# Long convolution and spectral mix: the filter's second transform is moved in front of the first pair's ticks

## The chip, the cores and the metric

One core of a Trainium2 chip runs the whole kernel. The metric is the device time of one execution in microseconds (us), the median of several runs. A profile of one further execution is shown; its time is given beside it. TensorE (PE in the profile, PEld for its weight loads) multiplies, VectorE (DVE) and ScalarE (ACT) empty PSUM and do elementwise work, GpSimd (POOL) and SyncE (SP) mainly issue DMAs.

## The reference

```python
# x: (8, 5696, 128), h: (5696, 128), w_r, w_i: (64, 128, 128), w_ch: (128, 128)
L = 2 * S
Yf = np.fft.rfft(x, n=L, axis=1) * np.fft.rfft(h, n=L, axis=0)[None]
x = np.fft.irfft(Yf, n=L, axis=1)[:, :S, :]          # causal long convolution
X = np.fft.rfft(x, axis=1)                           # spectral mix on the first 64 modes
Yr = einsum(Xr, w_r) - einsum(Xi, w_i);  Yi = einsum(Xr, w_i) + einsum(Xi, w_r)
u = x + np.fft.irfft(Y, n=S, axis=1)
out = u + np.maximum(u @ w_ch, 0.0)
```

## The kernel before, in words

**Tiling.** A sequence of 5696 is cut as 64 x 89 (J = 64, NQ = 89). A transform has two steps. The first step runs along the 89 and gives NK = 90 modes k. The second step runs along the 64, one small matrix per mode, out of the table `M`. The eight batches go in four pairs (`g_` = 0 to 3). The 90 modes of a pair go in NT = 23 ticks of KT = 4 modes (the last has 2).

**One pair.** First come 32 tiles of the first transform (`a_tile`, j = 0 to 31): four matmuls of x against the table F each, and one eviction of 128x720 from PSUM into `As`, on ACT or on DVE. The function `share` gives each eviction to the engine with the smaller sum of estimated costs. For the first pair all 32 tiles stand together; of a later pair the first six are spread over the last ticks of the pair before (`border`), and the other 26 follow those ticks. Then come the ticks (`tick`, t = 0 to 25), in which several steps overlap:

- `second(t)`: 16 matmuls `As` x `M` into two of the PSUM banks 0 to 3.
- `products(t)`: the product with the filter, `Hs`, on DVE. In most ticks ACT first copies the two banks to SBUF (`Xs`) and DVE multiplies from there.
- two ticks later (LC = 2), four matmuls `U` x `Wc` (banks 4 to 6), two ACT evictions into a room `Zs` or `Zt`, and one DMA of 256 KB from there to DRAM (`zscr`), issued on SP. The DMA has to land before the room is filled again.
- three ticks later (LM = 3), eight matmuls `Zs` x `G` (bank 7), which gather the 64 modes of the spectral mix.

During a pair's ticks GpSimd also issues the loads of x for the next pair (`x_load`, at the even ticks 2 to 16), and DVE puts them in place (`x_place`).

**Two forms of tick.** In the pairs after the first, `twin` makes the second transforms of two ticks stand together (32 matmuls in a row), and in every fourth tick (`straight`) DVE multiplies directly from PSUM without an ACT copy. The first pair has neither. It uses 6 rooms for its z tiles at the start, where the two middle pairs use 10 throughout.

**The filter.** Its first transform is made ahead of x (`Ah`). Its second transform is `filter_tick(t)`: 16 matmuls `Ah` x `M` with 64 columns, one eviction 128x512 to `Hs`, two DMAs of 64 KB on SP that copy `Hs` to its second plane with the partition halves exchanged, and after each odd t up to 11 one DMA of a piece of the table `G`, on SP too. Of the 23, the first six (LH = 6) are made among the first pair's tiles of x, one behind each third tile from j = 11 on. The others are made in the first pair's ticks, `filter_tick(t + 6)` at the end of tick t, in PSUM banks 2 and 3. That is why `second` of the first pair has only banks 0 and 1 until the filter is done.

**Queues.** Every engine runs its list strictly in the order in which the functions above are called. The recorder adds semaphore waits for data and for reuse. A DMA takes the next slot of a ring and waits until the slot's last DMA has landed; the ring of the `Hs` copies ("s") has 8 slots, that of the z writes ("z") 8, that of the `G` pieces 16. SP waits in its own list, so a copy that cannot go yet holds the z writes behind it.

**Fillers.** `keep(n, bank)` issues n matmuls whose result is not used: 12 behind the first pair's tiles, and 8 behind each of its ticks 0 and 1.

All matmuls are recorded at line 320, all DMAs at line 317, the evictions at 308 and 312 (plain, ACT and DVE) and 310 and 314 (scaled, ACT and DVE), the products at 592 and 600, `x_place` at 356. The profile's groups are therefore told apart by their tiles.

Of the kernel before, what the change touches and what calls it, by code (L numbers as in the profile page):

```python
# [123 lines left out]
def bass_long_conv_fft__then__afno_spectral_mix_kernel(nc, x, h, moe_w_r, moe_w_i, moe_w_ch, out):  # L124
# [8 lines left out]
    NP = B // 2  # L133
    KT = 4
    NT = (NK + KT - 1) // KT
# [15 lines left out]
    c, s = np.cos(th), np.sin(th)  # L151
# [75 lines left out]
    g_sb = at("G", GW, F16, a_g)  # L227
    ah_sb = at("Ah", HW, F16, a_g)
    NU, NXS, NZ, NZX = 3, 2, 6, 10
    NZS = [NZ] + [NZX] * (NP - 2) + [8]  # L230
    NZL = NZS[-1]
    a_st = take((2 * NU + NXS + NZ) * 2048)
    h_in = at("Hin", J * D, F16, a_st)
# [194 lines left out]
    def share(n):  # L428
        a, v = load["scalar"] + COST[n][0], load["vector"] + COST[n][1]
        e = "scalar" if a <= v else "vector"  # L430
        load[e] = min(a, v)
        return e
# [19 lines left out]
             [bank(t), bank(t + 1)], [("as", j)], 1.0 / 64, eng=eng, after=once(("hp", j), HP))  # L452


    def filter_tick(t, banks, eng="vector"):
        n = len(ticks[t])
        hb = banks
        for i, k in enumerate(ticks[t]):
            for r in range(2):
                for dh in range(2):  # L460
                    mm(pv(hb[dh], i * DH, [[1, DH]]),
                       ap(m_sb, MW, J * dh, J, k * 3 * J + (J if r == 0 else 0) + dh * J, [[1, P]]),
                       ap(ah_sb, HW, J * dh, J, (2 * k + r) * DH, [[1, DH]]), r == 0, r == 1,
                       AHT + mtok(k) + [("ag", k)], [bank(hb[dh])])
        lo, hi = KT * t * D, (KT * t + n) * D
        old = once("xr", [t_ for r_ in XR for t_ in r_]) if t == 0 else []
        evac(h_sb[:, lo:hi], pv(hb[0], 0, [[DH, n], [512, 2], [1, DH]]), [bank(hb[0]), bank(hb[1])], [("h", t, 0)],
             eng=eng, after=old)
        for p0, p1 in ((0, J), (J, 0)):
            dma("sync", h_sb[p0:p0 + J, HW + lo:HW + hi], h_sb[p1:p1 + J, lo:hi], "s", [("h", t, 0)], [("h", t, 1, p0)])  # L470
        if t % 2 and t // 2 < NG:
            s0, s1 = t // 2 * GP, min(t // 2 * GP + GP, NS)
            dma("sync", g_sb[:, s0 * P:s1 * P], bass.AP(c_g, s0 * P, [[GW, P], [1, (s1 - s0) * P]]), "c", (),
                [("g", t // 2)], after=[("ag", k) for k in range(s0, s1)])
# [62 lines left out]
    def keep(n, b0):  # L537
        for i in range(n):
            mm(pv(b0 + i % 2, 0, [[1, 2 * NK]]), f1_sb[:, 0:P], f1_sb[:, :], True, True, [("f1",)], [bank(b0 + i % 2)])

    LC, LM, LH = 2, 3, 6
    ZR = 96
    XBANKS = [bank(0), bank(1), bank(2), bank(3)]

    def with_h_at(g_, t):
        return g_ == 0 and t + LH < NT

    onchip = {}

# [5 lines left out]
        return e  # L555

    def twin(g_, t):
        return g_ > 0 and t % 2 == 1

    def straight(g_, t):  # L560
        return g_ > 0 and t % 4 == 3

    def slot_of(g_, t):
        if g_ == 0 or t == 0:
            return XSLOT[(t + 1) % 2 if t and not with_h_at(g_, t) else 0]
        return XSLOT[((t - 1) // 4 + t) % 2]

    def second(g_, t):
# [32 lines left out]
              bk + [("h", t, 0), ("h", t, 1, 0), ("h", t, 1, J)], [("u", i)])  # L601

    Z_OLD = [("ag", k) for k in range(NS, NS + 8 * (NZX - NZ))]
    XPLACE = [9, 10, 12, 15, 16, 18, 20, 22], [9, 10, 13, 14, 17, 18, 20, 22]

    def zroom(g_, s_):
        return (s_ - 2 * NZ) % NZX if g_ == 0 and s_ >= 2 * NZ else s_ % NZS[g_]

    def xtok(n):
        return [("xt", n, p_) for p_ in range(2)]  # L610
# [1 line left out]
    def tick(g_, t):  # L612
        if g_ + 1 < NP:
            for i in range(2 * XC):
                if t == XPLACE[g_ > 0][i]:
                    x_place(i, x_st[i], xtok(i))
        with_h = with_h_at(g_, t)
        if t < NT:
            of_two = t > 0 and twin(g_, t - 1)
            if not of_two and not (g_ == 0 and t > LC):  # L620
                second(g_, t)
            products(g_, t, slot_of(g_, t))
            if twin(g_, t):
                second(g_, t + 1)
                if straight(g_, t):
                    copied(g_, t + 1, slot_of(g_, t + 1))
        drain = list(border[t]) if t in border and g_ + 1 < NP else []
        if drain and t >= NT:
            j, sl, e = drain.pop(0)
            a_tile(j, [sl], e)  # L630
        if g_ + 1 < NP and t % 2 == 0 and 0 < t <= 4 * XC:
            i = t // 2 - 1
            x_load(g_ + 1, i, x_st[i], xtok(i), [("u", t % NU)] + AST)
        if LC <= t < NT + LC:
            s_ = t - LC
            n = len(ticks[s_])
            i, zi = s_ % NU, zroom(g_, s_)
            zb = [turns("z", ZBANK) for b in range(2)]
            for b in range(2):
                for r in range(2):  # L640
                    mm(pv(zb[b], 0, [[1, n * D]]), (W1, W2)[r], u_s[i][:, r * 1024 + b * 512:r * 1024 + b * 512 + n * D],
                       r == 0, r == 1, [("u", i), ("wc",)] + ([("u0", i)] if s_ == 0 and b else []), [bank(zb[b])])
                evac(bass.AP(z_s[zi], b * D, [[1024, P], [2 * D, n], [1, D]]),
                     pv(zb[b], 0, [[D, n], [1, D]]), [bank(zb[b])], [("zs", zi, b)], eng="scalar",
                     after=once(("zx", zi, b), Z_OLD) if zi >= NZ else ())
            zo = (g_ * NK + KT * s_) * P * 256
            dma("sync", bass.AP(zs, zo, [[256, P], [P * 256, n], [1, 256]]),
                bass.AP(z_s[zi], 0, [[1024, P], [256, n], [1, 256]]), "z",
                [("zs", zi, 0), ("zs", zi, 1)], [("zd", g_, s_)])
            if drain and t >= NT:  # L650
                j, sl, e = drain.pop(0)
                a_tile(j, [sl], e)
        if g_ == 0 and LC <= t < NT - 1:
            second(g_, t + 1)
        if LM <= t < NT + LM:
            s_ = t - LM
            zi = zroom(g_, s_)
            for b in range(2):
                for i, k in sorted(enumerate(ticks[s_]), key=lambda q: (s_ > 0 or q[1] != 1, q)):
                    if k % 2:  # L660
                        o, off, n, sl = pv(MB, b * P, [[1, P]]), (k + 1) // 2 * P, P, (k + 1) // 2
                    else:
                        ms, off = even[k]
                        n, sl = 2 * len(ms), 0
                        dims = [[M, 2]] if len(ms) == 1 else [[ms[1] - ms[0], 2], [M, 2]]
                        o = pv(MB, b * P + ms[0], dims)
                    mm(o, z_s[zi][:, i * 256 + b * P:i * 256 + b * P + P], g_sb[:, off:off + n],
                       k == 1 and b == 0, k == NK - 1 and b == 1, [("g", sl // GP), ("zs", zi, b)], [bank(MB)])
        if drain and t < NT + LM - 1:
            j, sl, e = drain.pop(0)  # L670
            a_tile(j, [sl], e)
        if with_h:
            filter_tick(t + LH, [2, 3])

    SLOTS = [0, 2, 4, 6]
    for j in range(32):
        a_tile(j, [turns("s", SLOTS)], "both" if j == 31 else share(720))
        if j >= 11 and j % 3 == 2 and (j - 11) // 3 < LH:
            b_ = turns("s", SLOTS)
            filter_tick((j - 11) // 3, [b_, b_ + 1], share(512))  # L680
    keep(12, turns("s", SLOTS))
    for g_ in range(NP):
        for t in range(NT + LM):
            tick(g_, t)
            if g_ == 0 and t < 2:
                keep(8, 4)
            assert g_ + 1 < NP or not wp
            if g_ == NP - 1 and t in early:
                pace[:] = [("u", min(t, NT - 1) % NU)]
                early[t]()  # L690
        evac(bass.AP(xt, 2 * g_ * XTW + M, [[B * XTW, P], [XTW, 2], [1, P]]), pv(MB, 0, [[P, 2], [1, P]]),
             [bank(MB)], [("xt", g_)], 1.0 / 64, eng="scalar", after=[("ag", k) for k in range(NS + 2 * XN, NK)])
        evac(bass.AP(xt, 2 * g_ * XTW, [[B * XTW, P], [XTW, 2], [1, M]]), pv(MB, M, [[P, 2], [1, M]]),
             [bank(MB)], [("xtn", g_)], -1.0 / 64, eng="vector" if g_ + 1 == NP else "scalar", after=[("ag", k) for k in range(NS + 2 * XN, NK)])
        if g_ + 1 < NP:
            for j in range(6, 32):
                a_tile(j, [(4, 6, 0, 2)[(j - 7) % 4] if j > 6 else 0], "both" if j == 31 else (A, V)[(j - 6) % 9 % 2])
                if j == 31:
                    keep(8, 6)
                if wp and j % 2 == 1:  # L700
                    dst, src_, ring, tok = wp.pop(0)
                    dma("gpsimd", dst, src_, ring, (), [tok], after=[("as", j)])
# [189 lines left out]
```

## Time and profile before

| | |
|---|---|
| median of 3 runs | 384.91 us (384.59 to 386.44) |
| profiled execution, its own time | 385.34 us |
| its span from first to last instruction | 383.2 us |
| PE, DVE, ACT, POOL busy | 96%, 81%, 79%, 22% of the span |
| granted TensorE clock | 0.99 |
| DMA | 103.94 MB, mean 271 GB/s |

The busy shares are means over stages with different limits. A PE marked busy is not one at its peak, since a matmul that stands in the pipeline behind a wait counts too. A stage's own length, and which work comes back at which distance in it, tell more. Times in the views count from the first instruction. The first pair's second transform begins at 43.88 us, those of the next pairs at 109.12, 164.28 and 219.06 us.

### The profile page before, as it was taken

To read this page: it belongs to the slowest core of one execution; us is meant where nothing else is said; L and a number is where in the kernel's file an instruction comes from. 1 tells how busy PE (TensorE), PEld (TensorE's weight loads), DVE (VectorE), ACT (ScalarE), POOL (GpSimd) and SP (SyncE) were. 2 spreads that over 40 slices of the span, in tenths; PEclk is the share of its full clock that TensorE was granted. 3 is DMA by queue.
4 is the path that set the end of the run, shared out by engine and by line. 5 is a ranking of instruction groups with operands and counts; after the bars stand their busy time and mean duration, and the time that the engine had idled before them with its cause. 6 is when DMAs were issued, how large, how long until landed. Compare 5 with 4: busy or idle time off the path is not lost.

```text
span 383.2 us, 12588 instructions
## 1 busy us (share of the span) xinstructions
PE 366.0 (96%) x5392; PEld 283.7 (74%) x5392; DVE 310.5 (81%) x348; ACT 302.7 (79%) x488; POOL 82.5 (22%) x133
## 2 busy tenths in 40 slices
PE   7999899999989999989999999999999999999994
PEld 7998756666866666866667866668898988887873
DVE  6969888998888999998998888875447767776876
ACT  1359688898889997989997999995457676776785
POOL 8400022220552320733310411319200000000000
PEclk9999999999999999999999999997999999999999
DMA  7998469999699997999995859999999999999879
GB/s 149 194 283 339 138 125 291 273 244 261 96 138 210 226 249 220 101 133 204 263 257 164 87 167 370 334 327 388 402 402 398 414 405 406 412 405 378 359 279 356
DMA packets 86865, 103.94 MB, mean 271 GB/s; under 512 B 22638, under 2 KB 72430, under 8 KB 83330
## 3 DMA queue, kind: packets, MB, share of 16 engines
q1 hardware_dynamic: 62523, 67.73, 50.5%
q0 software_dynamic: 24288, 35.43, 44.1%
q8 instruction: 42, 0.69, 0.7%
q14 instruction: 12, 0.10, 0.1%
HBM read 70.61 MB, written 51.12 MB: 318 GB/s over the span
## 4 chain that ended last, share of the span: by engine, by line
PE 69%; ACT 10%; DMA 9%; DVE 6%; POOL 2%; issue 2%; SPq 0%; DVEq 0%; POOLq 0%
PE ps L320 69%; ACT As L310 6%; DMA Xr<-in_x_dram 4%; DMA ZT0b<-zscr 4%; POOL Xr L317 2%; DVE As L314 2%; DVE U L592 1%; ACT UT L308 1%; ACT R L826 1%; ACT Zt L308 1%; DVE Xin L356 1%; ACT Xs L308 1%; DVE U L600 1%; DVE O L827 1%; DVE UT L312 0%
## 5 line engine op out<-in xcount | busy, mean ns | idle before, releaser
L600 DVE TENSOR_TENSOR U<-Xs,Hs 128x2048 f16<-128x2048 f16 (+1 forms) x73 | 86.7, 1190 | 12.0 <-ACT Xs L308 10.4
L320 PE MATMUL ps<-U,Wc 128*128 128x512 f16 (+1 forms) x368 | 94.0, 376 | 0.0
L308 ACT CAST Xs<-ps 128x1024 f16<-128x1024 f32 (+1 forms) x77 | 75.0, 979 | 9.0 <-PE ps L320 7.4
L308 ACT CAST Zs<-ps 128x512 f16<-128x512 f32 (+1 forms) x134 | 70.6, 596 | 5.9 <-PE ps L320 5.8
L827 DVE TENSOR_TENSOR O<-ps,R 128x512 f32<-128x512 f32 x81 | 52.6, 686 | 20.5 <-ACT R L826 15.2
L826 ACT ACTIVATE R<-ps 128x512 f32<-128x512 f32 x96 | 51.0, 573 | 14.2 <-PE ps L320 13.7
L314 DVE TENSOR_SCALAR As<-ps 128x720 f16<-128x720 f32 (+1 forms) x64 | 53.2, 880 | 5.1 <-PE ps L320 3.4
L320 PE MATMUL ps<-F,Xin 128*128 128x180 f16 x512 | 52.3, 250 | 2.6 <-DVE Xin L356 1.2
L320 PE MATMUL ps<-As,M 64*128 64x128 f16 x1440 | 50.6, 217 | 4.2 <-DVE U L592 3.0
L320 PEld LDWEIGHTS ps<-As,M 64*128 64x128 f16 x1440 | 40.3, 94 | 17.9 <-issue 8.1
L310 ACT ACTIVATE As<-ps 128x720 f16<-128x720 f32 x68 | 48.0, 768 | 6.4 <-PE ps L320 5.6
L320 PE MATMUL ps<-WI,UT 128*128 128x256 f16 x360 | 52.0, 279 | 0.5 <-DVE O L827 0.4
L320 PEld LDWEIGHTS ps<-F,Xin 128*128 128x128 f16 x512 | 44.5, 155 | 9.5 <-DVE As L314 2.6
L320 PEld LDWEIGHTS ps<-U,Wc 128*128 128x128 f16 x368 | 28.7, 97 | 27.6 <-ACT Zs L308 4.4
L317 POOL DMA_DIRECT2D Xt<-in_x_dram x48 | 26.0, 545 | 104.6 <-PE ps L320 100.2
L308 ACT CAST UT<-ps 128x712 f16<-128x712 f32 x40 | 30.0, 752 | 18.8 <-PE ps L320 17.8
L320 PEld LDWEIGHTS ps<-WI,UT 128*128 128x128 f16 x360 | 39.3, 152 | 4.4 <-issue 2.1
L320 PE MATMUL ps<-IBs,C 128*128 128x356 f16 x128 | 40.1, 323 | 0.6
L320 PEld LDWEIGHTS ps<-G,Zs 128*128 128x128 f16 x524 | 27.4, 96 | 11.7
L600 DVE TENSOR_TENSOR U<-ps,Hs 128x2048 f16<-128x2048 f32 x15 | 34.3, 2284 | 0.0
L320 PE MATMUL ps<-G,Zs 128*128 128x128 f16 (+2 forms) x524 | 32.6, 192 | 0.0
L320 PE MATMUL ps<-F 128*128 128x180 f16 x280 | 27.7, 254 | 2.5 <-DMA F<-cF 2.5
(86 smaller groups left out, 506.1 us busy)
## 6 DMA issues: line engine op xcount, KB each, us to landing
out_dram<-O SPq DMA_DIRECT2D x39, 512.0 KB, 11.4
zscr<-Zs SPq DMA_DIRECT2D x64, 256.0 KB, 6.8
Xt<-in_x_dram POOLq DMA_DIRECT2D x24, 320.0 KB, 7.0
zscr<-Zt SPq DMA_DIRECT2D x24, 256.0 KB, 6.6
W<-wscr POOLq DMA_DIRECT2D x4, 1024.0 KB, 8.9
M<-cM POOLq DMA_DIRECT2D x5, 720.0 KB, 20.5
ZT0a<-zscr SPq DMA_DIRECT2D x3, 1024.0 KB, 14.0
Hs<-Hs SPq DMA_DIRECT2D x44, 64.0 KB, 5.8
```

The costliest lines, as they stand in the source:

```text
L308: R.add(e, lambda h_: h_.copy(dst, src), reads, writes, after=after)
L310: R.add(e, lambda h_: h_.activation(dst, src, COPY, scale=scale), reads, writes, after=after)
L314: R.add(e, lambda h_: h_.tensor_scalar_mul(dst, src, scale), reads, writes, after=after)
L317: R.add(eng, lambda h_: h_.dma_start(dst, src), reads, writes, ring=ring, after=after)
L320: R.add("tensor", lambda h_: h_.matmul(o, l, r, start=st, stop=sp), reads, writes)
L356: R.add("vector", lambda e: e.tensor_copy(bass.AP(x_sb, i * XN * XS, [[XW, NQ], [XS, XN], [1, D]]), bass.AP(src, 0, [[XB, NQ], [D, XN], [1 ...
L592: R.add("vector", lambda e, b=b, s_=s_: e.tensor_tensor(bass.AP(u_s[i], b * 512, [[2048, P], [1024, 2], [1, n * D]]), s_, hv, MULT), [tok, ...
L600: R.add("vector", lambda e: e.tensor_tensor(uv, src, hv, MULT), bk + [("h", t, 0), ("h", t, 1, 0), ("h", t, 1, J)], [("u", i)])
L826: R.add("scalar", lambda e: e.activation(rv, src_r, RELU), bk, [("r", i % NR)], after=once(("r", i % NR), G_ALL + XTT + [("y", 0), ("y", 1 ...
L827: R.add("vector", lambda e: e.tensor_tensor(ov, src_u, rv, ADD), bk + [("r", i % NR)], [key + (h_,)], after=once(key, old))
```

## The change: what it does

All 23 filter ticks are now made among the first pair's 32 tiles of x: two at a time behind tiles 5, 7, 10, 12, 15, 17, 20, 22, 24, 27 and 29, and the last behind tile 30. Their evictions go to ACT or DVE by `share`, as before. No filter tick is left in the ticks, so banks 2 and 3 are free there, and the first pair's ticks take the later pairs' form: `twin`, `straight`, the same order of PSUM slots, the same places for x, 10 rooms for z. The fillers behind ticks 0 and 1 go, and those behind the tiles are 8 instead of 12.

```diff
-    NZS = [NZ] + [NZX] * (NP - 2) + [8]
+    NZS = [NZX] * (NP - 1) + [8]
...
-    LC, LM, LH = 2, 3, 6
+    LC, LM = 2, 3
...
-    def with_h_at(g_, t):
-        return g_ == 0 and t + LH < NT
...
     def twin(g_, t):
-        return g_ > 0 and t % 2 == 1
+        return t % 2 == 1
     def straight(g_, t):
-        return g_ > 0 and t % 4 == 3
+        return t % 4 == 3
     def slot_of(g_, t):
-        if g_ == 0 or t == 0:
-            return XSLOT[(t + 1) % 2 if t and not with_h_at(g_, t) else 0]
+        if t == 0:
+            return XSLOT[0]
         return XSLOT[((t - 1) // 4 + t) % 2]
...
-    XPLACE = [9, 10, 12, 15, 16, 18, 20, 22], [9, 10, 13, 14, 17, 18, 20, 22]
+    XPLACE = [9, 10, 13, 14, 17, 18, 20, 22]
     def zroom(g_, s_):
-        return (s_ - 2 * NZ) % NZX if g_ == 0 and s_ >= 2 * NZ else s_ % NZS[g_]
+        return s_ % NZS[g_]
...
-            if not of_two and not (g_ == 0 and t > LC):
+            if not of_two:
                 second(g_, t)
...
-        if g_ == 0 and LC <= t < NT - 1:
-            second(g_, t + 1)
...
-        if with_h:
-            filter_tick(t + LH, [2, 3])
     SLOTS = [0, 2, 4, 6]
+    done = 0
     for j in range(32):
         a_tile(j, [turns("s", SLOTS)], "both" if j == 31 else share(720))
-        if j >= 11 and j % 3 == 2 and (j - 11) // 3 < LH:
+        due = NT if j == 30 else max(0, j - 2) * NT // 28 // 2 * 2
+        while done < due:
             b_ = turns("s", SLOTS)
-            filter_tick((j - 11) // 3, [b_, b_ + 1], share(512))
-    keep(12, turns("s", SLOTS))
+            filter_tick(done, [b_, b_ + 1], share(512))
+            done += 1
+    keep(8, turns("s", SLOTS))
     for g_ in range(NP):
         for t in range(NT + LM):
             tick(g_, t)
-            if g_ == 0 and t < 2:
-                keep(8, 4)
```

More of the change, by code (lines that the diff above doesn't have):

```diff
@@ L452, in a_tile, with filter_tick @@
              [bank(t), bank(t + 1)], [("as", j)], 1.0 / 64, eng=eng, after=once(("hp", j), HP))
-    def filter_tick(t, banks, eng="vector"):
+    def filter_tick(t, banks, eng):
         n = len(ticks[t])
@@ L614, in tick @@
             for i in range(2 * XC):
-                if t == XPLACE[g_ > 0][i]:
+                if t == XPLACE[i]:
                     x_place(i, x_st[i], xtok(i))
-        with_h = with_h_at(g_, t)
         if t < NT:
             of_two = t > 0 and twin(g_, t - 1)
-            if not of_two and not (g_ == 0 and t > LC):
+            if not of_two:
                 second(g_, t)
```

## The prediction, made before the changed kernel was run

> **What bounds the kernel now.** I read the busy time by windows first, with a window for the first pair's tiles and one for each pair from its first `second` to the next pair's.
>
> ```profile
> core 0: us, PE busy (x) PEld busy (x) DVE busy (x) ACT busy (x) POOL busy (x), PEclk, DMA share, GB/s
> 27.96:43.88 15.92, 15.76 (x236) 13.78 (x237) 14.58 (x19) 14.54 (x20) 0.00 (x0) 1.00 0.78 284
> 43.88:109.12 65.24, 63.34 (x1048) 42.72 (x1050) 56.48 (x66) 55.88 (x87) 17.41 (x28) 1.00 0.93 203
> 109.12:164.28 55.16, 53.10 (x768) 37.74 (x769) 50.98 (x49) 50.81 (x82) 17.17 (x29) 1.00 1.02 193
> 164.28:219.06 54.78, 52.82 (x769) 37.73 (x770) 50.99 (x49) 50.80 (x82) 15.53 (x26) 1.00 0.97 190
> ```
>
> The first pair takes 65.24 us, the next two 55.16 and 54.78. The clock is 1.00 in all, so the 10 us are work and order, not the clock. The timeline of PE shows where they lie. Three excerpts follow: first-pair ticks with a filter tick, first-pair ticks without one, and two ticks of the second pair.
>
> ```profile
> 57.28 0.41 PE L320 MATMUL ps<-Ah,M 64*128 64x64 f16 x16
> 57.62 1.04 PE L320 MATMUL ps<-U,Wc 128*128 128x512 f16 x4
> 58.59 0.62 PE L320 MATMUL ps<-As,M 64*128 64x128 f16 x16
> 59.14 0.50 PE L320 MATMUL ps<-G,Zs 128*128 128x2 f16 x8
> 59.57 0.41 PE L320 MATMUL ps<-Ah,M 64*128 64x64 f16 x16
> ...
> 86.44 1.02 PE L320 MATMUL ps<-U,Wc 128*128 128x512 f16 x4
> ...
> 88.28 1.02 PE L320 MATMUL ps<-U,Wc 128*128 128x512 f16 x4
> ...
> 119.59 1.07 PE L320 MATMUL ps<-As,M 64*128 64x128 f16 x32
> 120.59 1.04 PE L320 MATMUL ps<-U,Wc 128*128 128x512 f16 x4
> ...
> 123.11 1.07 PE L320 MATMUL ps<-As,M 64*128 64x128 f16 x32
> ```
>
> The first column is the start. A tick with a filter tick comes back after 59.57 - 57.28 = 2.29 us, one without after 88.28 - 86.44 = 1.84, and in the twin form two ticks after 123.11 - 119.59 = 3.52, or 1.76 each. PE stands nearly closed up in the first, so the filter's matmuls there lie on the path.
>
> The tiles of x are different: both eviction engines are full there, as the timelines of ACT and DVE show.
>
> ```profile
> 28.55 14.68 ACT L310 ACTIVATE As<-ps 128x720 f16<-128x720 f32 x20 [3.12 <-PE ps L320]
> ...
> 33.18 0.69 DVE L312 CAST Hs<-ps 128x512 f16<-128x512 f32 x1
> 33.96 0.91 DVE L314 TENSOR_SCALAR As<-ps 128x720 f16<-128x720 f32 x1
> 34.78 0.68 DVE L312 CAST Hs<-ps 128x512 f16<-128x512 f32 x1
> ```
>
> ACT runs 20 evictions without a gap, DVE alternates with gaps under 0.1 us. PE could do a tile in 4 x 0.078 = 0.31 us (the spacing of the filler matmuls, 2.35 us for 30 weight loads), but the tiles come at 0.397 (12 tiles in 32.73 - 27.97 = 4.76 us). The evictions set this stage.
>
> **What leaves the ticks.** Filter ticks 6 to 22 leave 17 ticks of the first pair: 17 x (2.29 - 1.76) = 9.0 us. The six ticks that had none gain 6 x (1.84 - 1.76) = 0.5. The rest is the start, where the first pair has two fillers of 0.79 us, filter ticks and waits between its first `second` and its second `U,Wc` block (43.88 to 50.60, 6.7 us) and the second pair does the same in 4.5 us (109.12 to 113.58). Three filter ticks of that stretch are counted already. The windows give the total without such counting: 65.24 - 55.16 = **10.1 us less** (10.5 by the third pair). The work of the two pairs in that window is otherwise the same: as many x loads, z writes, placed pieces, tiles and pieces of w.
>
> **What the tiles of x get.** Sixteen full filter ticks and one of half size. Five groups of one filter tick and three tiles take 7.60 us (32.73 to 40.33 in the same timeline), 1.52 each; less 3 x 0.397 = 1.19 that is 0.33 for a filter tick. 16.5 x 0.33 = **5.4 us more**. Bounds: if `share` fills both engines evenly, a filter eviction costs what the two do side by side. ACT takes 0.54 for a 128x512 (1.08 for two z evictions) and DVE 0.69, together one in 0.30, which gives 5.0. If PE with its two banks per filter tick becomes the longer part, a filter tick costs what it costs in the ticks without the twin form, 2.29 - 1.84 = 0.45, which gives 7.4. I take 0.33, since it is measured in this stage with the same neighbours. So the first `second` comes at 43.88 + 5.4 = 49.3.
>
> **What the table M allows.** The filter reads M earlier. Its six pieces are issued at 10.69 to 13.32 and land 18.1, 19.3, 20.5 up to 25.7 us later: the first at 28.8, the second at 30.5, the last at 39.0. Filter ticks 0 and 1 now stand behind six tiles, at 27.97 + 6 x 0.397 = 30.4. Tick 3, which needs the second piece, comes at 27.97 + 8 x 0.397 + 3 x 0.33 = 32.1, and tick 18, which needs the last, at about 45. No wait; its cost would be at most the 1.6 us by which the first piece is ahead, should its order change.
>
> **What moves on SP.** Of the 46 copies of `Hs` 30, issued from 51.71 on, and the last two of the six G pieces move in front of the first z write. A pair of copies takes 1.13 us of SP, a G piece 0.64 with its gap, as the timeline of SP has it.
>
> ```profile
> 51.71 1.13 SPq L317 DMA_DIRECT2D Hs<-Hs  x2
> ...
> 55.01 0.59 SPq L317 DMA_DIRECT2D G<-cG  x1
> ```
>
> All of them: 23 x 1.13 + 6 x 0.64 = 29.8 us. The first copy follows its first matmul by 33.91 - 32.73 = 1.2 us, so SP starts at 31.5 and is free at 61.3 if nothing else holds it. The ring of 8 does hold it wherever a copy takes over 8 x 0.565 = 4.5 us to land. By the rows of the tile `Hs`, copies issued from 31 to 50 us land after 1.9 to 5.4 (median 3.1), those from 51 to 87, beside loads of x and z writes, after 4.8 to 8.2 (median 6.3).
>
> ```profile
> DMA to landing us min/median/max: 1.9/3.1/5.4
> DMA to landing us min/median/max: 4.8/6.3/8.2
> ```
>
> Ten copies at 5.4 while M arrives (0.67 each), twenty at SP's own 0.565, sixteen beside the x loads at 5.6 (0.70), somewhat under the 6.3 since no z writes are out then: 29.2 in place of 26.0, so SP is free at about 64.5. The first z write, which in the second pair goes 4.6 us into the pair, goes 15 us into it. Ten rooms make that free up to a point: the eleventh z tile is evicted 129.56 - 109.12 = 20.4 us into the pair, here at 69.7. The first write lands at 64.5 + 3.3 (the 51.15 one took 3.3) = 67.8. That cover is 1.9 us deep; at the 7.1 that is the median of the second pair's z writes the stall is 1.9. ACT would wait there, and behind it the copies for DVE. I take 0 and keep 1.9 for the range. The products do not wait: a tick's copies go out every 1.3 us or so from 31.5 on, the ticks come every 1.76 from 49.3 on.
>
> How copies fare beside long transfers decides the depth of that cover. The copy issued at 33.91 took 5.4 and landed at 39.3, just behind the last piece of M at 39.0: beside a long transfer of the other queue a copy waits. [...]
>
> **Without cost.** Four fillers fewer behind the tiles: they end at 43.73, before the last eviction of `As` at 43.82, so nothing stood behind them. The fillers in ticks 0 and 1 are in the 10.1 already. The second and third pair run at clock 1.00 without them.
>
> **Sum.** -10.1 + 5.4 = -4.7 us. The profiled execution took 385.34, so 380.6 on its scale. It lay 0.43 above the median of 384.91; on the median's scale the forecast is **380.2 us**. What follows only moves forward: the later pairs and the output stage hang on the pair before, not on absolute times.
>
> **Rivals.**
>
> *The z writes come late (slower).* If all 46 copies land in L us with L over 4.5, the ring sets their pace: SP is free at 31.5 + 3.8 + 46 L / 8, the first z write lands 3.3 later, and the stall at the eleventh z tile is 5.75 L - 31.1. It starts at L = 5.4, eats the 4.7 us at L = 6.2, and at L = 7.0 is 9.2 us: 389.4. For it: 6.3 is the median beside x loads, and 8.2 occurs. Against: until the x loads begin, some 5 us into the ticks, the bus has only M's end, copies and G, and copies in such a stretch (41.4 to 50) landed within 3.2. Chance 0.12, half of it beyond "no change".
>
> *The tiles pay more.* Filter ticks come in twos with one eviction each and hold two of four PSUM slots. At 0.45 each the gain is 10.1 - 7.4 = 2.7: 382.2. For it: PE's own 0.31 + 0.34 per tile and filter tick is close to the evictions' 0.70, so each waits for the other at times. Against: the measured 0.33. Chance 0.13.
>
> *The first pair does not reach 55.2 because of its transfers.* DMA share by length is 0.93 x 65.24 = 60.7 in the first pair and 1.02 x 55.16 = 56.3 in the second: copies and G are worth 4.4 us of the bus. About half of them now fall into the ticks, and the z writes in a block behind them. If the bus decides, 2.2 us come back through late pieces of x (DVE waits in `x_place`): 382.4; with the stall of 1.9 it is 384.3. Against: no wait for pieces of x stands among the second pair's waits, although its bus is as full. Chance 0.08.
>
> *It does not do what it says,* M being late or the order of slots holding the twin form back: about 384.9. Nothing in the trace asks for it; chance 0.02.
>
> **How the numbers follow.** The forecast has 0.65. The bound for a difference is 0.5%, 1.9 us: faster is under 383.0, slower over 386.8. Faster: 0.65, 0.11 of the dearer tiles and 0.04 of the transfers, 0.80. Slower: 0.06 of the late z writes and 0.01 of the rest, 0.07. No change: 0.13. The range: -10.5 + 5.0 with 0.9 for what the shorter start may add gives 384.91 - 6.4 = 378.5; above, 7.4 in the tiles and 1.9 of stall, 384.91 - 10.1 + 7.4 + 1.9 = 384.1. Outside lie the larger part of the late z writes and some below.
>
> **What would show it.** Right: the first `second` near 49.3, the next pair's near 104.4, two ticks in 3.5 us, copies of `Hs` in a row on SP to about 64, the first z write near there, and no wait on ACT before the eleventh z tile. Wrong: an ACT gap near 69.7 with a DMA `zscr` as releaser (late z writes); a first `second` after 51 (dearer tiles); DVE waiting for `Xt` (transfers).

## The result, and the profile after

The changed kernel takes 389.54 us (median of 4 runs, 389.04 to 389.87) against 384.87 us before (with one run more than in the table above): a ratio of 1.0103, 95% interval 1.0084 to 1.0122. The forecast was 380.2, so the sign is wrong. The profiled execution took 389.34 us, its span is 387.2. Among the profiled executions below, the output stage behind the pairs was longer than here by 6 us in e3, 4 in the repeat of the changed kernel and 2 in e2, so of these only the earlier stages are read.

Busy time by windows, after, with the same cuts as before: the tiles, then each pair from its first `second` on. The columns are the window, its length, busy time and instructions of each engine, granted clock, DMA share and GB/s.

```profile
27.89:50.13 22.24, 21.39 (x496) 18.15 (x497) 19.36 (x25) 19.12 (x31) 0.00 (x0) 1.00 0.75 260
50.13:112.16 62.03, 54.49 (x768) 38.13 (x768) 51.15 (x49) 50.77 (x82) 16.85 (x28) 0.94 0.94 195
112.16:167.31 55.15, 52.82 (x770) 37.73 (x770) 51.06 (x49) 50.80 (x82) 17.22 (x29) 1.00 1.01 193
167.31:222.96 55.65, 52.96 (x769) 37.76 (x770) 51.09 (x49) 50.98 (x82) 15.58 (x26) 1.00 0.98 188
```

The tiles grew from 15.92 to 22.24 us (+6.3), the first pair shrank from 65.24 to 62.03 (-3.2) instead of to 55.2, the third pair is 0.9 longer, the rest is equal within 0.1: together +4.0, as the spans have it (387.2 - 383.2). The first pair has the same PE, DVE and ACT work as the second but 7 us more of time, and its clock is 0.94. ACT's timeline after shows where:

```profile
69.61 1.08 ACT L308 CAST Zt<-ps 128x512 f16<-128x512 f32 x2
77.66 1.07 ACT L308 CAST Zs<-ps 128x512 f16<-128x512 f32 x2 [6.97 <-DMA zscr<-Zs]
```

This is the eleventh z tile. Its room is the first, and the first z write has not landed. SP's timeline after shows why:

```profile
31.27 2.44 SPq L317 DMA_DIRECT2D Hs<-Hs  x4
...
53.24 16.88 SPq L317 DMA_DIRECT2D Hs<-Hs  x22
70.16 7.96 SPq L317 DMA_DIRECT2D zscr<-Zs  x6
```

The first z write leaves SP at 70.16, behind the last of 46 copies, and lands 7.4 us later. Everything behind ACT stops with it, PE for 5.58 us. Two windows around the end of the stop show what that does to the clock:

```profile
72.00:78.30 6.30, 0.72 (x10) 0.13 (x5) 0.99 (x2) 0.64 (x2) 1.04 (x2) 0.71 0.98 212
78.30:81.80 3.50, 3.50 (x22) 1.78 (x22) 1.98 (x3) 3.50 (x6) 0.00 (x0) 0.54 1.03 285
```

PE comes back to a clock of 0.54 after its stop of 5.58 us, and from 81.80 on it is 1.00. It costs little this time: the two ticks around the stop take 81.86 - 71.12 = 10.74 us where two ticks take 3.5, so 0.3 more than the wait itself.

### The profile page after: what moved, and what is told of

Read it like the earlier page. It is cut to its first block, busy times and chain, and to the rows that moved or that the text cites. A ratio compares the mean times of both kernels' runs of the same rounds, so it can differ in the third digit from the quotient of the medians.

```text
span 387.2 us, 12544 instructions
## 1 busy us (share of the span) xinstructions
PE 362.1 (94%) x5372; PEld 283.1 (73%) x5372; DVE 310.1 (80%) x337; ACT 302.3 (78%) x494; POOL 82.4 (21%) x133
## 4 chain that ended last, share of the span: by engine, by line
PE 66%; ACT 12%; DMA 11%; DVE 5%; POOL 2%; issue 2%; SPq 0%; DVEq 0%; ACTq 0%; POOLq 0%
PE ps L320 66%; ACT As L310 6%; DMA Xr<-in_x_dram 4%; DMA ZT0b<-zscr 4%; DVE As L314 2%; POOL Xr L317 2%; DMA zscr<-Zs 2%; ACT R L819 2%; ACT Zt L308 1%; DVE U L589 1%; ACT UT L308 1%; ACT Xs L308 1%; DVE Xin L356 1%; DVE UT L312 0%; DVE O L820 0%
## 5 line engine op out<-in xcount | busy, mean ns | idle before, releaser
L320 PE MATMUL ps<-U,Wc 128*128 128x512 f16 (+1 forms) x368 | 95.6, 380 | 6.3 <-ACT Zs L308 5.6
L597 DVE TENSOR_TENSOR U<-Xs,Hs 128x2048 f16<-128x2048 f16 (+1 forms) x68 | 80.7, 1189 | 18.0 <-ACT Xs L308 15.4
L308 ACT CAST Xs<-ps 128x1024 f16<-128x1024 f32 (+1 forms) x72 | 69.5, 971 | 7.5 <-PE ps L320 5.3
L308 ACT CAST Zs<-ps 128x512 f16<-128x512 f32 (+1 forms) x126 | 66.1, 596 | 10.5 <-DMA zscr<-Zs 7.0
L314 DVE TENSOR_SCALAR As<-ps 128x720 f16<-128x720 f32 (+1 forms) x67 | 55.9, 881 | 6.1 <-PE ps L320 4.5
L320 PE MATMUL ps<-As,M 64*128 64x128 f16 x1440 | 48.5, 217 | 4.5 <-DVE U L589 3.5
L310 ACT ACTIVATE As<-ps 128x720 f16<-128x720 f32 (+1 forms) x65 | 46.0, 767 | 8.2 <-PE ps L320 7.0
L597 DVE TENSOR_TENSOR U<-ps,Hs 128x2048 f16<-128x2048 f32 x20 | 45.7, 2283 | 0.0
L308 ACT CAST Zt<-ps 128x512 f16<-128x512 f32 (+1 forms) x58 | 30.9, 603 | 0.0
L320 PE MATMUL ps<-G,Zs 128*128 128x2 f16 (+2 forms) x492 | 30.8, 193 | 0.0
```

The costliest lines, as they stand in the source:

```text
L308: R.add(e, lambda h_: h_.copy(dst, src), reads, writes, after=after)
L310: R.add(e, lambda h_: h_.activation(dst, src, COPY, scale=scale), reads, writes, after=after)
L314: R.add(e, lambda h_: h_.tensor_scalar_mul(dst, src, scale), reads, writes, after=after)
L320: R.add("tensor", lambda h_: h_.matmul(o, l, r, start=st, stop=sp), reads, writes)
L597: R.add("vector", lambda e: e.tensor_tensor(uv, src, hv, MULT), bk + [("h", t, 0), ("h", t, 1, 0), ("h", t, 1, J)], [("u", i)])
```

## The experiments

**Theories.** Queue: the z writes stand behind the copies on SP, and the room is free too late. Bus: the transfers of the shorter pair are too many, in whatever order. Tiles: the dearer tiles are the loss. Each ratio below is to the kernel before on the same chip, with its 95% interval. A profile shows one execution; the times are medians of several.

**z writes off SP (e10).** The first pair's z writes are issued by GpSimd, so they also change their DMA queue and their ring ("q", 10 slots). The copies stay on SP, in the same order.

```diff
-            dma("sync", bass.AP(zs, zo, ...), ..., "z",
+            dma("sync" if g_ else "gpsimd", bass.AP(zs, zo, ...), ..., "z" if g_ else "q",
```

> The changed kernel with nothing moved on SP: the 46 copies and the G pieces stay as they are, but the first pair's z writes are issued by GpSimd. Queue theory: each z write goes out when its tile is ready (the first near 55), no wait for a room, first pair 55 to 56 us, 382 to 383 us in all. If instead the bus holds the writes (copies, x and z together from 53 to 70 us, as in e1), the first pair takes 58 us or more.

Measured: 381.34 us, ratio 0.9891 (0.9868 to 0.9914). The first pair in its windows, then SP's and GpSimd's timelines of e10:

```profile
50.00:105.50 55.50, 53.16 (x770) 37.89 (x772) 51.09 (x49) 50.91 (x82) 36.30 (x51) 1.00 0.90 217
```

```profile
53.16 17.98 SPq L317 DMA_DIRECT2D Hs<-Hs  x22
```

```profile
56.45 1.57 POOL L317 DMA_DIRECT2D zscr<-Zs  x2
```

The copies keep SP busy to 71.1, as long as in the changed kernel, and the same bytes cross the bus; only the z writes go out from 56.45 on instead of 70.16. They land no faster there: the first takes 5.3 us, and 8.4 is the median of the first 14. No wait for a room is left, and the first pair takes 55.5 us. The queue theory stands, and the bus theory falls as an account of the 7 us. The tile theory falls too: the tiles still take 21.8 us, and the kernel is faster than the one before.

**Two rooms fewer (e6).**

```diff
-    NZS = [NZX] * (NP - 1) + [8]
+    NZS = [8] + [NZX] * (NP - 2) + [8]
```

> The changed kernel with 8 z rooms in place of 10 for the first pair. Queue theory: the first z write leaves SP at the same 70.2 us, but the ninth z tile needs its room two ticks earlier, so ACT waits 2 x 1.75 = 3.5 us longer, 10.5 in place of 7.0, and the first pair takes 62.0 + 3.5 = 65.5 us; 393 us in all. If the room was not what ACT waited for, no change.

Measured: 392.98 us, ratio 1.0178 (1.0131 to 1.0224). ACT's timeline of e6:

```profile
77.96 1.07 ACT L308 CAST Zs<-ps 128x512 f16<-128x512 f32 x2 [10.41 <-DMA zscr<-Zs]
```

10.4 us of wait where 10.5 were expected; the first z write leaves at 70.20, and the first pair takes 66.3 us (65.5 expected). It is the room.

**Sixteen slots (e4).** The ring of the copies gets 16 slots in place of 8.

> The changed kernel with 16 ring slots for the copies in place of 8. It tells how much of SP's 38.9 us from the first copy to the first z write is waiting for slots (by the issue times about 2.7 us at 38 to 40 and 1.6 us at 65 to 70) and how much SP's own issuing. If the slots are the small part: first z write near 66, stall 2.5 to 4, 385.5 to 387 us. If they are the main part: first z write before 63, no stall, 382.5.

Measured: 385.06 us, ratio 0.9984 (0.9945 to 1.0024). SP's timeline of e4:

```profile
52.74 15.57 SPq L317 DMA_DIRECT2D Hs<-Hs  x22
68.35 9.00 SPq L317 DMA_DIRECT2D zscr<-Zs  x6
```

The first z write comes 1.8 us earlier, where some 4 were expected; the waits for a room are 6.1 us in two pieces, and the first pair takes 60.7. The slots are the small part; SP's own issuing is the large one. The first pair agrees with that, though the median gained more than these 1.3 us. The profiled execution took 387.47 us, one of the longer of the ten; what the shorter ones did is not shown.

**The copies in the ticks (e1, e9).** In e1 only the copies of ticks 0 to 5 stay among the tiles, and those of tick t + 6 are issued at the end of tick t. e9 does the same with one double copy for two ticks.

```diff
# e1 (in e9 with one copy for ticks t + 6 and t + 7, at even t)
+        if g_ == 0 and t + 6 < NT:
+            h_copy(t + 6)
```

> All filter ticks stay among the tiles of x, but only the copies of Hs for ticks 0 to 5 are issued there; those of tick t + 6 are issued on SP at the end of the first pair's tick t, behind that tick's z write, as in the kernel before. The work, the bytes and the order on PE, ACT and DVE are those of the changed kernel. Queue theory (the 44 copies that stand on SP in front of the first z write hold it until 70.2 us, and the eleventh z tile waits 7.0 us for its room): first z write near 55, no wait of ACT for zscr, first pair 55.2 us long, 389.5 - 7.0 = 382.5 us. Bus theory (the bus is too full with copies, x and z for the shorter pair, whatever the order): the wait only moves, 386 us or more. Tile theory (the dearer tiles, 6.2 us, are the loss): under 1 us gained.

> e1 with one copy of 128 KB for two ticks: the copies of ticks t + 6 and t + 7 on SP at the end of the even tick t. In e1 no z room was waited for, but the first pair still took 59.5 us, with products and pieces of x late. SP theory (in e1 SP has 1.9 to 2.4 us of issuing per tick of 1.75, two copies and one z write, and is itself the bound): half the copies to issue, first pair near 55 to 56 us. Bus theory (z writes, x and copies together are more than the bus moves in the shorter ticks): the same bytes, first pair 58 to 60 us.

Measured: e1 386.01 us, ratio 1.0000 (0.9969 to 1.0030); e9 389.26, ratio 1.0105 (1.0046 to 1.0164). No wait for a room in either, but the first pair takes 59.5 and 58.9 us. So e1 missed the 382.5 of the queue theory and came out at the 386 that the bus theory had set. In e1 a piece of x comes 1.0 us late and copies 0.9; in e9 copies come 2.5 us late, and e9 loses 3.1 us more in the tiles, as told below for e2. Half the issues shortened the first pair by only 0.6 us, and some of them were long, as SP's timeline of e9 shows for two copies:

```profile
69.12 4.45 SPq L317 DMA_DIRECT2D Hs<-Hs  x2
```

So six ticks ahead is not early enough beside x and the z writes. Whether the bus or SP's stretched issuing holds them back is not separated by these two. The same bytes, with the copies well ahead of their use, go through in 55.5 us in e10, so these bytes alone do not make the pair long.

**One copy for two ticks among the tiles (e2), and the copies on GpSimd (e3).**

```diff
# e2
-        for p0, p1 in ((0, J), (J, 0)):
-            dma("sync", ..., "s", [("h", t, 0)], [("h", t, 1, p0)])
+        if t % 2 or t == NT - 1:
+            for p0, p1 in ((0, J), (J, 0)):
+                dma("sync", ..., "s", ...)          # both ticks' columns
# e3
-            dma("sync", h_sb[...
+            dma("gpsimd", h_sb[...
```

> The copies stay among the tiles, but one copy of 128 KB serves two filter ticks, which come in twos anyway: 24 in place of 46, with the same bytes. Queue theory: SP needs 24 x 0.6 + 6 x 0.64 = 18 us, less than the filter ticks last (31 to 49), so it is free near 52, the first z write goes out when its tile is ready, 382.5 us. If SP's time goes with bytes, not with the number of copies (long issues, ring slots held twice as long), the first z write stays at 66 to 70 and the gain is under 3 us. Bus theory: no or little gain, since the bytes are the same.

> The 46 copies are issued by GpSimd, whose queue is empty from 14 us to the first x load of the ticks at 55; the ring of 8 stays. Queue theory: SP has only the G pieces, the first z write goes out near 55, no wait for a room, 382.5 us; GpSimd is done with the copies at about 31.3 + 46 x 0.55 = 57 to 62, so the first loads of x come up to 7 us later, which they can bear (x is placed from tick 9 on). Bus theory: 386 or more.

Measured: e2 386.51 us, ratio 1.0005 (0.9977 to 1.0032); e3 384.93, ratio 0.9958 (0.9927 to 0.9989). The first pair came out as the queue theory said, 54.8 us in e2 and 56.2 in e3, without a wait for a room. Part of the gain was lost elsewhere: the tiles stage takes 3.1 us more than in the changed kernel in e2, and 2.4 more in e3. PE's timeline of e2, in the middle of a tile, and two windows behind it:

```profile
41.50 0.70 PE L320 MATMUL ps<-F,Xin 128*128 128x180 f16 x6
44.67 0.46 PE L320 MATMUL ps<-F,Xin 128*128 128x180 f16 x2 [2.48 <-issue]
```

```profile
41.50:45.00 3.50, 1.02 (x10) 0.76 (x8) 1.45 (x2) 0.69 (x2) 0.00 (x0) 0.90 0.94 256
45.00:48.40 3.40, 3.40 (x77) 2.94 (x76) 2.02 (x3) 2.26 (x4) 0.00 (x0) 0.60 0.98 260
```

PE stops for 2.48 us, waiting for nothing that the profile shows, and then has a clock of 0.60. The same place, in the second tile after filter ticks 12 and 13, has a stop of 1.60 us in e3, 2.31 in e9, 0.40 in the changed kernel and 0.35 in e4. The DMA view has one transfer of 16 KB of the kind "instruction" near it, which starts at 42.0 in e2 and at 39.6 in the changed kernel. In all five traces with the stop the matmuls resume 1.4 to 1.6 us after this transfer ends, however long they stood. Copies issued up to 41 us took 7.6 to 9.3 us to land in e2.

**The double copies behind M (e5, and again).**

```diff
# e2, and the copies read the last piece of M's token
-                    [("h", t_, 0) for t_ in range(t0, t + 1)], ...)
+                    [("h", t_, 0) for t_ in range(t0, t + 1)] + [("m", MP - 1)], ...)
```

> One copy of 128 KB for two filter ticks, as in e2, but the first copy waits until the last piece of M has landed (38 to 39 us). In e2 the first pair's ticks took 54.8 us, and the loss was a stop of PE of 2.5 us among the tiles, at 42, that ends with the arrival of a block of its instructions, and a half clock behind it. Fetch theory (copies beside M fill the bus, the copies land 9 us late and the block of instructions comes late with them): no stop of PE near 42, first second transform at 50 as in the changed kernel, first pair 54.8 us, in sum 4.2 us less than the kernel before in the profile (about -1.1%). If the stop has another cause (the table of 128 KB copies, chance), it stays: no difference from before.

> e5 again, as the measure for e8 on the same chip: 1.1 to 1.3% faster than before, first pair 54.8 us, no wait for a room.

Measured: 381.39 us, ratio 0.9879 (0.9845 to 0.9914), and 382.23, ratio 0.9913 (0.9893 to 0.9932). Its windows:

```profile
27.90:50.10 22.20, 21.54 (x506) 18.36 (x508) 19.26 (x25) 19.17 (x31) 0.00 (x0) 1.00 0.74 256
50.10:105.00 54.90, 52.95 (x779) 37.86 (x775) 50.99 (x49) 50.80 (x82) 17.20 (x29) 1.00 1.00 221
```

The stop is gone and the clock is 1.00 (the cut at 105.00 lies 0.1 behind the next pair's start; pair to pair it is 54.8). The copies start at 38.9, and the first three land after 2.2 to 4.1 us. The 16 KB transfer starts at 37.45. So the copies beside M caused the stop; that it was the block of instructions that they delayed is argued from its place and time, not shown alone. The expectation has the stop end with the arrival of the block; in e2 the transfer ends at 43.13 and the matmuls resume at 44.67. The first z write goes out at 61.1, some six microseconds after its tile, and the rooms cover it.

**Filter ticks singly (e8).** e5 with `due = ... * NT // 28` without the rounding to twos.

> e5 with the filter ticks one by one among the tiles in place of two at a time. The tiles stage took 6.0 to 6.3 us more than before where 5.4 were forecast. If the excess comes from two filter ticks standing together in the four PSUM slots, the stage gets 0.5 to 0.9 us shorter, 380.5 to 381; if the evictions set the stage, no difference from e5.

Measured: 381.95 us, ratio 0.9908 (0.9886 to 0.9929), so no difference from e5. The tiles are not shorter but 0.9 us longer in the profile (22.8 against 21.9). That two ticks stand together is not what the tiles pay for.

**The fillers back (e7), and the changed kernel again.**

> The changed kernel with the fillers of the kernel before: 12 behind the tiles and 8 behind each of the first pair's ticks 0 and 1. The prediction held them to be free. Then the wait for the room is shorter by what they delay the eleventh z tile and the time is the same, 389 to 390. If they kept the clock up among the ticks, no half clock is left besides that in the wait at 75, and the time falls by up to 1 us; if they lie on the path, the ticks 0 and 1 come 1.2 us later, which the wait for the room swallows.

> The changed kernel once more, beside the others of this call on one chip and against the same runs of the kernel before. Every theory: 1.0 to 1.3% slower than before, first pair 62 us with one wait of ACT for a z room of about 7 us; the time itself may differ by 1 us from the first result, as the kernel before did between calls.

Measured: e7 388.29 us, ratio 1.0062 (1.0028 to 1.0096); the changed kernel again 388.39, ratio 1.0074 (1.0046 to 1.0103), a little under the 1.0 to 1.3% that was expected. The first pairs are 61.9 and 63.1 us long, against 62.0. With the fillers the time is the same as without, but the tenth z tile comes 0.6 us later, and the waits for a room are 4.8 us in place of 7.0. So what the fillers cost can be hidden in the wait, as the expectation said. In the repeat the wait for the room is 7.3 us, and the third pair takes 54.9 us: the 0.9 us that it was longer in the first profile, a piece of x 0.8 late, is not part of the change.

## Why the prediction was wrong, by its steps

**Which case came.** The first rival, late z writes, which had 0.12. The prediction had the wait at the right tile and from the right DMA ("an ACT gap near 69.7 with a DMA `zscr` as releaser"; it ran from 70.7 to 77.7), and took 0 for it.

**The term that failed: what moves on SP.** Two sizes in it were wrong. SP was to be free at 64.5 and was at 70.2: 38.9 us for the copies and G pieces in place of 33.0. A pair of copies was priced at 1.13 us, from one of the shortest rows of SP's timeline of before. The same timeline has longer ones soon after, and these were passed over:

```profile
56.31 1.63 SPq L317 DMA_DIRECT2D Hs<-Hs  x2
...
58.66 1.91 SPq L317 DMA_DIRECT2D Hs<-Hs  x2
...
61.80 2.27 SPq L317 DMA_DIRECT2D Hs<-Hs  x2
```

The fifteen pairs from 51.71 on there take 1.53 us in the mean. In the changed kernel the 46 issues take 29.5 us in all where 26.0 were priced, the G pieces 3.5, and the gaps between the issues 5.8. The prediction had 3.2 for waits on slots, and e4 shows that more slots save only 1.8. And the first z write was to land in 3.3 us, as the first one before did. That row was an exception: the next z write before, at 52.88, took 7.4. The first one after the change took 7.4, near the 7.1 that the prediction had for the second pair and kept for the range. Together: 5.7 late on SP, 4.1 late on the bus, less 1.9 of cover and 0.8 because the pair itself began later, gives 7.1 for a wait of 7.0.

**The rival's own price** put the delay on the ring's slots, with every copy at 6.6 us for 7 us of wait. The copies took 5.0 in the median; the place was right, the mechanism of the price was not. A cover of 1.9 us rested on terms that were off by 5.7 and 4.1; its failing should have been given more than 0.12.

**The ticks:** 10.1 us less was right. Where nothing waits for a room and the copies go out among the tiles, the first pair takes 54.8 (e2, e5) to 56.2 us (e3), against 65.24 before. With the copies in the ticks (e1, e9) it does not get there.

**The tiles:** 5.4 us were forecast; 6.3 came, of which 0.40 is the stop told above, and 6.0 in the repeat, which has no such stop. Both lie inside the bounds of 5.0 and 7.4. e8 speaks against the ticks in twos as the reason; what the other 0.6 is stays open.

**M, fillers, products:** right but for details. M held no filter tick back. Leaving the fillers out lost nothing, but e7 does not show what they cost, since the wait for the room hides it. One product waited 0.7 us for its copy in the changed kernel.

**The traffic:** the row that the prediction trusted (the copy at 33.91, 5.4 us) was borne out. The first four copies after the change took 6.8 to 7.8 us and landed at 38 to 41, about when M's last piece did (40). So the copies issued beside M landed late in these rows too. The rival of late pieces of x did not come: no piece was waited for in the changed kernel's first pair.

**The sum without the failed term:** e10 and e5 keep the change and free the z writes; their ratios of 0.9891, 0.9879 and 0.9913 stand near the forecast, 380.2 / 384.91 = 0.988, with tiles somewhat dearer than forecast. Both beat both kernels.

## What to carry to other kernels

When a step is moved, walk the issuing queue too: every DMA that it issues moves with it, and what stood behind it on that queue, here a write that frees a buffer (70.16 us, against 51.15 before), is late by all of them. Price a DMA issue and a landing from the mean of many rows, not from one short row, and treat a cover thinner than the uncertainty of its terms as a coin's toss. Where a queue must carry both, give the write that frees rooms another queue (e10), or bundle the early copies and hold them back until the long load has landed (e5); bundling alone (e2) gained nothing in all.

## What the runs showed of the hardware that was not expected

PE stopped in these runs without any semaphore wait that the profile shows. With copies beside the last pieces of M it stood 1.6 to 2.5 us in the middle of a tile (128 KB copies in e2 and e9, 64 KB copies from GpSimd in e3), and with the copies behind M (e5) it did not stop. The granted clock then fell: it was 0.60 over the 3.4 us from 45.0 on in e2, 0.57 from 44.5 to 48.0 in e3, and 0.50 from 44.21 to 47.60 in e9. So stops of 1.60 us (e3), 2.31 (e9) and 2.48 (e2) came before the lower clock; behind the stop of 0.40 us in the changed kernel it was 1.00 (42.30 to 45.70).

The page of the changed kernel counts 42 transfers of the kind "instruction" on queue q8, 0.69 MB in all, some 16 KB each. Seven of them fall between 30 and 72 us, and in that stretch PE has one stop for which the profile shows no wait (0.40 us). That one of these transfers was waited for in the runs with the stop is an estimate from its place and time; no run shows it alone.

Most issues of one copy on SP took 0.46 to 0.60 us in the changed kernel, but now and then one took up to 2.1 us (3.8 in e9). A full bus alone does not explain it: the three longest of the changed kernel's copies (1.14, 1.50 and 2.09 us, at 44.26, 47.91 and 55.02) stood while the DMA share was 0.43 to 0.48, and the one of 3.8 us in e9 while it was 1.11. What holds SP there is open.
